# Pooled attention with a cosine router on one core: where GpSimd's drain stands, when the flagged batches are counted, and how the second pass is skipped

## The chip, the core and the metric

The kernel runs on one core of a Trainium2 chip. Its time is the device time of one execution in microseconds (us). A core has TensorE for matrix products (PE in the rows; PEld is its weight loads), VectorE (DVE), ScalarE (ACT), GpSimd (POOL) and SyncE (SP), each with its own queue of instructions, and 16 DMA engines. GpSimd's queue issues the loads of q, k, v and of the weights; SyncE's queue issues nearly all stores. A name that ends in q (POOLq, PEldq) is the sequencer of that engine, which carries out branches, waits, register loads and drains.

## The reference, cut

Attention over 8 batches, 8 heads, 576 rows of 64, in which keys and values are first averaged over groups of 8 (72 keys are left); its result is the input of a router that sends each of the 4608 rows to one of 8 experts.

```python
k_p = k.reshape(B, H, Sp, pool, D).mean(axis=3)       # Sp = 72, pool = 8
v_p = v.reshape(B, H, Sp, pool, D).mean(axis=3)
attn = softmax(scale * q @ k_p^T)
x = (attn @ v_p).transpose(0, 2, 1, 3).reshape(4608, 512)
logits = normalized(x) @ normalized(expert_emb).T / tau
expert_idx = np.argmax(logits, axis=1)                # one of 8 experts a row
gate_w = softmax(logits)[row, expert_idx]
out[mask] = gate_w[mask, None] * (np.maximum(x[mask] @ w1[e], 0.0) @ w2[e])
```

w1[e] is 512 x 1024 and w2[e] 1024 x 512.

## The kernel before, in words

A batch is one unit of work. For each of the 8 batches the kernel forms the attention, transposes its result to xt, and routes it. Before the routing is known it guesses one expert for the whole batch: `choose` (names GD, with FIND_INDEX8 as its last instruction) writes the index of the guessed expert to ix_all, `pick` (PK, L359) reads that index into a register of GpSimd's queue, and `load_w1` and `load_w2` (W1 on L343, W2 on L349) fetch that expert's weights. The products with w1 are `h_mm` (H, L707), those with w2 are `y_mm` (Y0 to Y3 of a batch, L719) and `yl_mm` (YL, the last 64 rows, L725). The rows are scaled with their gate while they leave PSUM (YE on L731, YF and YG for YL, L733 and L731) and stored (L337). W10 below means w1 of batch 0, W20 w2 of batch 0; V2 is the load of v of batch 2, Y7.2 the third product with w2 of batch 7, and so on.

Rows whose expert is not the guessed one, or whose values are out of a range, are caught by a second pass. `presence` sets this up in three steps: PR on VectorE (the range), PP on TensorE (one product of ones_m with ohb, the one-hot choices of all batches, `present`), and PX on VectorE (`extra`, 8 short instructions, L872 to L884), which write a flag for each batch (flag_i) and n_i, which is 8 if any flag is set and 0 otherwise. The program then reads n_i into a register of all five engines (L997) and runs a loop from 0 to n_i (L998). With these inputs n_i is 0 and the loop's body isn't run.

The order of the work is made before the program is built: every step is added to a plan with the engines that may run it, a busy time and a priority; the planner (`Plan.order`) places steps one at a time, by the earliest start and then the priority (for batch b it is b times PERIOD, 21, and some more, with a table of tuned corrections). GpSimd's loads have a written order of their own: V0, K0, Q0, V1, then PK0, W10, K1, Q1, W20, V2, NA0 (the root of batch 0's norms, L398), PK1, W11 and so on. Some stores wait until a load named for them has landed; `landing` holds what they wait for. While TensorE would wait early on, the planner puts products without use ahead (`keep_warm`, L813). The steps are issued in this order inside `tc.manual_schedule()`. What stands after that block is placed by a scheduler:

```python
    nc.gpsimd.drain()                                              # L996
    n_val = nc.values_load(n_i[0:1, 0:1], min_val=0, max_val=B)    # L997, all engines
    with tc.For_i(0, n_val, 1) as i:                               # L998
```

The scheduler put the drain of L996 far ahead of its place in the text: on GpSimd's queue it stands right behind the load V1 and ahead of PK0.

At the loop's end each engine jumps out of the loop, takes down the counters that it raised itself, and waits for the counters of the others; then a barrier over all engines ends the program (L1078).

Of the kernel before, what the change touches and what calls it, by code (L numbers as in the profile page):

```python
# [16 lines left out]
ALU = mybir.AluOpType  # L17
AX = mybir.AxisListType
ENG = mybir.EngineType
# [194 lines left out]
def kernel(  # L214
# [520 lines left out]
    def chunk_rows(o_b, c):  # L735
        return o_b[ts(c, 128)]
# [241 lines left out]
    for b in range(B):  # L978
        xt = Buf(xt_r)
        attention(b, b * PERIOD, xt)  # L980
        ffn(b, (b + 1) * PERIOD, xt)
    presence(B * PERIOD + 8.0)

    with tc.manual_schedule():
        order = plan.order(loads)
        first = [s for s in order if s.name in ("V0.0", "V0.1", "K0.0", "K0.1")]
        for s in first:
            s.run()
        prelude()
        for s in order:  # L990
            if s not in first:
                if s.fill:
                    keep_warm(s.fill_on, s.fill)
                s.run()

    nc.gpsimd.drain()  # L996
    n_val = nc.values_load(n_i[0:1, 0:1], min_val=0, max_val=B)  # L997
    with tc.For_i(0, n_val, 1) as i:  # L998
        f_val = nc.values_load(flag_i[0:1, ds(i, 1)], min_val=0, max_val=1)
        with tc.If(f_val > 0):  # L1000
            of = lambda t: t[ds(i, 1)].squeeze(0)
            o_b = out[ds(i * S, S)]
            xt = xt_r.tiles[0]
            attend_again(of(q), of(k), of(v), xt)
            y, o = y_r.tiles[0], y_r.tiles[1]
            nc.vector.memset(y, 0.0)
            for c in range(4):
                nc.sync.dma_start(out=chunk_rows(o_b, c), in_=y)
            put_last(o_b, y)
            w1, w2 = w1_r[0].tiles[0], w2_r[0].tiles[0]  # L1010
            with tc.For_i(0, E, 1) as e:
                p_val = nc.values_load(pick_i[0:1, ds(e, 1)], min_val=0, max_val=1)
                with tc.If(p_val > 0):
                    load_w1(e, w1)
                    load_w2(e, w2)
                    gmx = ssq_all[:, 0]
                    nc.vector.tensor_copy(out=gmx, in_=oh_x[:, :, ds(e, 1)].squeeze(2))
                    nc.vector.tensor_tensor(out=gmx, in0=gmx, in1=gate_all[:, B], op=ALU.mult)
                    hT = hT_r.tiles[0:8]
                    for w in range(8):  # L1020
                        for j in range(2):
                            p = (bank.tiles + psum.tiles)[(2 * w + j) % 4]
                            h_mm(xt, w1, w, j * HALF, (j + 1) * HALF, p)
                            h_relu(p, hT[w], j * HALF, (j + 1) * HALF, 'ACT' if j else 'DVE')
                    gl = gl_all[:, B:B + 1]
                    nc.vector.tensor_copy(out=gl, in_=gmx[64:128, 4:5])
                    for c in range(5):
                        p = (bank.tiles + psum.tiles)[c % 4]
                        if c < 4:
                            y_mm(hT, w2, c, p[:, 0:DM])  # L1030
                            scale_rows(y, p[:, 0:DM], gmx[:, c:c + 1], 'DVE')
                            dst, cols = chunk_rows(o_b, c), DM
                            nc.sync.dma_start(out=o, in_=dst)
                        else:
                            yl_mm(hT, w2, p)
                            for r in range(2):
                                rows = ts(r, 64)
                                scale_rows(y[rows, 0:DH], p[rows, ts(r, DH)],
                                           gmx[rows, 4:5] if r else gl, 'DVE')
                                nc.sync.dma_start(out=o[rows, 0:DH], in_=last_rows(o_b)[r])  # L1040
                            cols = DH
                        nc.vector.tensor_tensor(out=y[:, 0:cols], in0=y[:, 0:cols],
                                                in1=o[:, 0:cols], op=ALU.add)
                        if c < 4:
                            nc.sync.dma_start(out=dst, in_=y)
                        else:
                            put_last(o_b, y)


# [33 lines left out]
```

## Time and profile before

| | us |
|---|---|
| median of 3 runs | 209.63 (208.03 to 210.13) |
| the profiled execution | 210.25 |
| its span, from first to last recorded instruction | 208.5 |
| TensorE busy in it | 192.2 (92%) |
| VectorE, ScalarE, GpSimd busy | 140.6, 136.6, 43.0 |
| granted TensorE clock, mean over the span | 0.971 of full speed |

The profile is of one execution. Times in its rows are us from the start of the span, so an instruction "at 29.38" starts 29.38 us in. The profiled execution's own time is 1.75 us longer than its span; that part lies outside the recorded instructions. In brackets at the end of a row stands how long the engine sat idle before it and what ended that idle time.

### The profile page before, as it was taken

How to read it: one execution, taken by the hardware profiler on the slowest of the kernel's cores; microseconds unless marked ns; L12 is line 12 of the kernel's file. 1: busy time of each engine (PE TensorE's matmuls, PEld its weight loads, DVE VectorE, ACT ScalarE, POOL GpSimd, SP SyncE). 2: the span in 40 equal slices, each digit the busy share in tenths (PEclk: the TensorE clock that was granted, in tenths of full speed). 3: DMA queues.
4: the chain of work that ended last, by engine and by line, in shares of the span. 5: the costliest groups of instructions: out<-in, count | busy, mean ns of one | idle time of the engine just before them, and what ended most of it. 6: DMA issues, size and time to landing. Idle time of an engine off the chain costs nothing.

```text
span 208.5 us, 5415 instructions
## 1 busy us (share of the span) xinstructions
PE 192.2 (92%) x2080; PEld 125.2 (60%) x2081; DVE 140.6 (67%) x409; ACT 136.6 (65%) x313; POOL 43.0 (21%) x59
## 2 busy tenths in 40 slices
PE   7979989899999989999999999999999999999910
PEld 5745568447765667557765676566756676586410
DVE  2355389837896898669998897879997476242130
ACT  3004876857978779767975778469967878385410
POOL 7301603603400703006201510043000600020000
PEclk9966999999999999999999999999999999999995
DMA  4992899999999999999999999989996799950330
GB/s 56 183 183 36 137 205 212 206 207 187 207 206 176 204 211 196 209 206 210 249 208 212 177 246 242 228 173 249 239 219 232 145 218 230 267 208 3 128 104 6
DMA packets 27839, 38.71 MB, mean 186 GB/s; under 512 B 4248, under 2 KB 14488, under 8 KB 27808
## 3 DMA queue, kind: packets, MB, share of 16 engines
q0 software_dynamic: 21904, 28.85, 82.4%
q1 hardware_dynamic: 5824, 9.39, 13.3%
q8 instruction: 18, 0.29, 0.6%
q14 instruction: 13, 0.11, 0.2%
q10 hardware_dynamic: 80, 0.07, 0.1%
HBM read 61.88 MB, written 9.44 MB: 342 GB/s over the span
## 4 chain that ended last, share of the span: by engine, by line
PE 55%; DMA 24%; issue 7%; POOL 4%; DVE 4%; ACT 2%; POOLq 1%; SPq 0%; DVEq 0%; ACTq 0%
PE pb L707 20%; PE pb L719 15%; DMA kr<-in_k_dram 11%; DMA vr<-in_v_dram 10%; PE pa L589 3%; PE pa L719 3%; PE pa L707 3%; PE pa L634 3%; PE pb L378 2%; DMA out_dram<-y 2%; PE pb L725 2%; POOL vr L319 2%; PE pb L387 1%; DVE vr L448 1%; ACT y L731 1%
## 5 line engine op out<-in xcount | busy, mean ns | idle before, releaser
L707 PE MATMUL pb<-xt,w 128*128 128x288 f16 (+2 forms) x432 | 61.3, 287 | 0.9 <-DMA w<-in_moe_w_dram 0.9
L707 PEld LDWEIGHTS <-w 128*128 128x128 f16 x512 | 47.0, 98 | 16.2 <-issue 4.6
L719 PE MATMUL pb<-w,hT 128*128 128x512 f16 x224 | 52.6, 379 | 0.9 <-DMA w<-in_moe_w_dram 0.9
L597 ACT ACTIVATE at<-pa 72x576 f16<-72x576 f32 (+2 forms) x64 | 38.2, 642 | 5.2 <-PE pa L589 4.8
L719 PEld LDWEIGHTS <-hT 128*128 128x128 f16 x256 | 23.2, 97 | 26.1 <-issue 2.4
L655 ACT ACTIVATE sq<-x 128x512 f16<-128x512 f16 x40 | 25.2, 630 | 13.6 <-DVE x L370 8.7
L713 ACT ACTIVATE hT<-pb 128x288 f16<-128x288 f32 (+2 forms) x74 | 28.6, 411 | 6.9 <-PE pb L707 4.9
L731 ACT ACTIVATE y<-pb,gm_all 128x512 f32<-128x512 f32 (+1 forms) x30 | 19.0, 634 | 14.9 <-PE pb L719 11.0
L370 DVE TENSOR_TENSOR x<-pa,r_all 128x512 f16<-128x512 f32 x38 | 26.3, 691 | 2.1
L548 DVE STREAM_TRANSPOSE qT<-qq 128x576 f16<-128x576 f16 x32 | 23.2, 755 | 1.3 <-DMA qq<-in_q_dram 1.3
L398 POOL TENSOR_TENSOR ssq_all<-ssq_all,half_c 128x5 f32<-128x5 f32 x8 | 10.4, 1294 | 47.1 <-ACT sq L655 47.1
L715 DVE TENSOR_SCALAR hT<-pb 128x288 f16<-128x288 f32 (+2 forms) x34 | 14.9, 447 | 7.2 <-PE pb L707 6.9
L349 POOL DMA_DIRECT2D w<-in_moe_w_dram x8 | 5.5, 688 | 65.3 <-PE pb L725 17.0
L448 DVE TENSOR_TENSOR vr<-vr 72x2048 f16<-72x2048 f16 (+1 forms) x16 | 15.1, 942 | 5.2 <-DMA vr<-in_v_dram 5.2
L813 PE MATMUL pb<-ones_m 128*128 128x256 f16 x102 | 17.1, 314 | 1.4 <-DVE half_c L820 1.4
L589 PE MATMUL pa<-qT,kpT 32*72 32x288 f16 (+2 forms) x256 | 15.7, 295 | 0.1
L378 PEld LDWEIGHTS <-x 128*128 128x128 f16 x160 | 10.8, 97 | 6.7 <-DVE x L370 3.0
L378 PE MATMUL pb<-ident_h,x 128*128 128x128 f16 x144 | 13.5, 219 | 1.4 <-DVE x L370 1.2
L634 PEld LDWEIGHTS <-at 72*128 72x128 f16 x320 | 13.1, 98 | 1.9 <-issue 0.3
L634 PE MATMUL pa<-vpx,at 72*128 72x65 f16 x304 | 14.2, 194 | 0.0
L448 DVE TENSOR_TENSOR kr<-kr 72x2048 f16<-72x2048 f16 (+1 forms) x14 | 13.2, 944 | 1.2 <-DMA kr<-in_k_dram 1.1
L650 ACT COPY xt<-pb 128x512 f16<-128x512 f16 (+1 forms) x25 | 13.0, 536 | 0.7 <-PE pb L378 0.5
(115 smaller groups left out, 200.2 us busy)
## 6 DMA issues: line engine op xcount, KB each, us to landing
w<-in_moe_w_dram POOLq DMA_DIRECT2D x16, 1024.0 KB, 17.8
out_dram<-y SPq DMA_DIRECT2D x32, 256.0 KB, 6.1
vr<-in_v_dram POOLq DMA_DIRECT2D x7, 576.0 KB, 20.0
kr<-in_k_dram POOLq DMA_DIRECT2D x7, 576.0 KB, 18.0
qq<-in_q_dram POOLq DMA_DIRECT2D x7, 576.0 KB, 16.8
out_dram<-y SPq DMA_DIRECT2D x15, 64.0 KB, 6.3
qq<-in_q_dram POOLq DMA_DIRECT2D x2, 288.0 KB, 8.9
vr<-in_v_dram POOLq DMA_DIRECT2D x1, 512.0 KB
```

What stands on the lines that cost most here:

```text
L370: nc.vector.tensor_tensor(out=x[:, ts(i, np_)], in0=pxv[:, :, 1:129].rearrange("p a (r d) -> p a r d", d=D), in1=rv.unsqueeze(3).to_broadc ...
L378: nc.tensor.transpose(out=pt.bitcast(FP16)[:, ts(w, 128)], in_=xf[:, ts(w, 128)], identity=ident_h)
L448: nc.vector.tensor_tensor(out=t[:, :, 0:m], in0=t[:, :, 0:m], in1=t[:, :, m:2 * m], op=ALU.add)
L548: nc.vector.transpose(out=qT.tile[:, a].rearrange("p t c e -> p (t c e)")[:, cols], in_=qq.tile[:, a, cols]),
L589: nc.tensor.matmul(out=tiles[m // 2].tile[0:gs, m % 2 * 512:m % 2 * 512 + (p1 - p0) * T], lhsT=kpT.tile[ts(m, R), a, c, 0:gs], rhs=qT.tile ...
L597: nc.scalar.activation(out=t.tile[:, :, p0 * T:p1 * T].rearrange("g r (p t) -> g r p t", t=T), in_=p.tile[0:G].rearrange("g (r c) -> g r c ...
L634: nc.tensor.matmul(out=px[h // 2 // np_].tile[:, o:o + 65], lhsT=at[h // 2].tile[:, h % 2, c0:c0 + 128], rhs=vp.tile[:, h // 2, 1 + h % 2 ...
L655: nc.scalar.activation(out=sq, in_=x.tile.rearrange("p a r d -> p (a r d)"), func=AF.Square, accum_out=ssq_all[:, b, c:c + 1])
L707: nc.tensor.matmul(out=p[:, 0:c1 - c0], lhsT=w1v[:, kk, w // 2, w % 2, :], rhs=xt[:, kk, c0:c1], start=(kk == 0), stop=(kk == 3))
L713: nc.scalar.activation(out=dst, in_=src, func=AF.Relu)
L719: nc.tensor.matmul(out=p, lhsT=hT[w][:, ts(c, 128)], rhs=w2[:, w // 2, w % 2, :], start=(w == 0), stop=(w == 7))
L731: nc.scalar.activation(out=dst, in_=src, func=AF.Copy, scale=g)
```

## The change: what it does

1. The drain stands inside `manual_schedule`, as the last thing in it. On GpSimd it now comes behind the last load and the last NA, directly ahead of the reading of n_i. (The listing of instructions below leaves drains out, so this move can't be seen in it: GpSimd's rows from V1 to PK0 read alike before and after.)
2. `presence` is given a base of B * PERIOD - 200 where it was B * PERIOD + 8, so that its steps have a higher priority than most others that are ready.
3. The second pass stands under `tc.If(n_val > 0)` with its body laid out as the fall-through, and its loop runs from 0 to 8. When n_i is 0 an engine branches to the else-side of the condition, where it takes down its own counters and branches on to the end. Waits for the other engines' counters stand in that side only for SyncE, 12 of them; before, each engine had 12 or 13.
4. A hint with the branch's place ("again") is put on TensorE's queue behind the product Y7.1 (`landing["Y1"]` is overwritten batch by batch, so it is batch 7's).
5. The reading of n_i on SyncE moves ahead of the last three stores.

```diff
     def y_mm(hT, w2, c, p):
         for w in range(8):
-            nc.tensor.matmul(out=p, lhsT=hT[w][:, ts(c, 128)], rhs=w2[:, w // 2, w % 2, :],
-                             start=(w == 0), stop=(w == 7))
+            landing[f"Y{c}"] = nc.tensor.matmul(
+                out=p, lhsT=hT[w][:, ts(c, 128)], rhs=w2[:, w // 2, w % 2, :],
+                start=(w == 0), stop=(w == 7))
...
-    presence(B * PERIOD + 8.0)
+    presence(B * PERIOD - 200.0)
...
                 s.run()
-
-    nc.gpsimd.drain()
+        nc.gpsimd.drain()
+
+    with tc.issue_after(landing["Y1"].ins):
+        tc.mark_branch_hint_location("again", engines=[ENG.PE])
     n_val = nc.values_load(n_i[0:1, 0:1], min_val=0, max_val=B)
-    with tc.For_i(0, n_val, 1) as i:
-        f_val = nc.values_load(flag_i[0:1, ds(i, 1)], min_val=0, max_val=1)
...
+    with tc.If(n_val > 0, preferred_fallthrough_block=True, label="again"):
+        with tc.For_i(0, B, 1) as i:
+            f_val = nc.values_load(flag_i[0:1, ds(i, 1)], min_val=0, max_val=1)
...
```

**TensorE, batch 7's last products.** PP (the product with ohb) stands before behind YL7, the last product of all (hT are the hidden values, w the weights, pa and pb banks of PSUM):

```order
L725 LDWEIGHTS hT_102
L725 MATMUL pb_63<-w_74,hT_102 64x256
L869 LDWEIGHTS ones_m
L869 MATMUL pb_65<-ohb,ones_m 128x328
L997 TENSOR_LOAD n_i
L998 COMPARE_AND_BRANCH
```

After, it stands between Y7.0 (bank pb_64) and Y7.1 (bank pa_62):

```order
L719 LDWEIGHTS hT_99
L719 MATMUL pb_64<-w_74,hT_99 128x512
L719 LDWEIGHTS hT_102
L719 MATMUL pb_64<-w_74,hT_102 128x512
L870 LDWEIGHTS ones_m
L870 MATMUL pb_66<-ohb,ones_m 128x328
L719 LDWEIGHTS hT_103
L719 MATMUL pa_62<-w_74,hT_103 128x512
```

The hint stands between Y7.2 (bank pa_61) and Y7.3 (bank pb_63):

```order
L719 LDWEIGHTS hT_102
L719 MATMUL pa_61<-w_74,hT_102 128x512
L1082 BRANCH_PREFETCH_HINT
L719 LDWEIGHTS hT_103
L719 MATMUL pb_63<-w_74,hT_103 128x512
```

So PP went up by four products, and one instruction of the queue is new.

**VectorE, behind the gates of batch 7** (L693 is the last of them). Before, YF7, which scales half of YL7, stands ahead of the 8 instructions of PX:

```order
L693 TENSOR_TENSOR gm_all<-gm_all,gate_all 128x5
L733 TENSOR_SCALAR y_115<-pb_63,gl_all 64x256
L872 TENSOR_REDUCE pos_all<-pb_65 1x64
L875 TENSOR_SCALAR pos_all<-pos_all 1x64
L877 TENSOR_TENSOR ext<-pos_all,eb_all 1x64
L878 TENSOR_REDUCE flag<-ext 1x8
L879 SCALAR_TENSOR_TENSOR flag<-pb_65,flag 1x8
L882 TENSOR_SCALAR flag_i<-flag 1x8
L883 TENSOR_REDUCE anyf<-flag 1x1
L884 TENSOR_SCALAR n_i<-anyf 1x1
L997 TENSOR_LOAD n_i
```

After, PX stands ahead of YF7:

```order
L693 TENSOR_TENSOR gm_all<-gm_all,gate_all 128x5
L873 TENSOR_REDUCE pos_all<-pb_66 1x64
L876 TENSOR_SCALAR pos_all<-pos_all 1x64
L878 TENSOR_TENSOR ext<-pos_all,eb_all 1x64
L879 TENSOR_REDUCE flag<-ext 1x8
L880 SCALAR_TENSOR_TENSOR flag<-pb_66,flag 1x8
L883 TENSOR_SCALAR flag_i<-flag 1x8
L884 TENSOR_REDUCE anyf<-flag 1x1
L885 TENSOR_SCALAR n_i<-anyf 1x1
L734 TENSOR_SCALAR y_115<-pb_65,gl_all 64x256
L1000 TENSOR_LOAD n_i
```

PX no longer stands behind a wait for YL7.

**SyncE, the last stores.** y_112 is stored for Y7.0, y_122 for Y7.1, y_121 and y_120 for Y7.2 and Y7.3, y_115 for half of YL7. Before:

```order
L337 DMA out_dram<-y_112 128x512
L337 DMA out_dram<-y_122 128x512
L337 DMA out_dram<-y_121 128x512
L337 DMA out_dram<-y_120 128x512
L337 DMA out_dram<-y_115 64x256
L997 TENSOR_LOAD n_i
L997 ISA x2
L998 COMPARE_AND_BRANCH
```

After:

```order
L337 DMA out_dram<-y_112 128x512
L337 DMA out_dram<-y_122 128x512
L1000 TENSOR_LOAD n_i
L1000 ISA x2
L337 DMA out_dram<-y_121 128x512
L337 DMA out_dram<-y_120 128x512
L337 DMA out_dram<-y_115 64x256
L1001 COMPARE_AND_BRANCH
```

The reading of n_i moved ahead of three stores, each of which waits for its rows to be scaled.

## Rows read from the trace of the kernel before

**Rows 1.** The page: engines, granted clock, DMA, chain by engine:

```profile
PE 192.2 (92%) x2080; PEld 125.2 (60%) x2081; DVE 140.6 (67%) x409; ACT 136.6 (65%) x313; POOL 43.0 (21%) x59
...
PEclk9966999999999999999999999999999999999995
DMA  4992899999999999999999999989996799950330
...
PE 55%; DMA 24%; issue 7%; POOL 4%; DVE 4%; ACT 2%; POOLq 1%; SPq 0%; DVEq 0%; ACTq 0%
```

**Rows 2.** The drain's line, L996 (duration in ns, start in us):

```profile
L996 POOLq DRAIN  x1: 14163/14163/14163, 4.6 to 4.6; - x1
```

**Rows 3.** DMA issues of 0 to 8 us (KB each, median us to landing):

```profile
vr<-in_v_dram POOLq DMA_DIRECT2D x1, 576.0 KB, 12.2
```

**Rows 4.** The chain of waits, 0 to 30 us (start, us, what):

```profile
6.27 0.86 POOL vr L319
7.13 11.69 issue
18.82 0.48 POOLq L359
...
23.41 21.73 DMA vr<-in_v_dram
```

**Rows 5.** VectorE in order of time, 9 to 12 us:

```profile
11.13 0.17 DVE L524 FIND_INDEX8 ix_all<-mx_all,pb 128x8 uint32<-128x8 f32 x1
```

**Rows 6.** Line L343, the loads of w1 of two batches, 18 to 50 us:

```profile
L343 POOL DMA_DIRECT2D w<-in_moe_w_dram x2: 793/805/817, 20.3 to 35.9; - x2
...
DMA to landing us min/median/max: 9.0/9.0/9.0
```

**Rows 7.** Stretches: busy time of PE, PEld, DVE, ACT, POOL; PEclk; DMA share; GB/s:

```profile
18.50:21.20 2.70, 2.65 (x26) 1.09 (x25) 0.85 (x2) 1.98 (x4) 0.89 (x2) 0.95 0.00 0
...
35.90:39.90 4.00, 4.00 (x44) 2.43 (x41) 3.93 (x11) 3.44 (x9) 3.97 (x5) 1.00 1.17 209
```

**Rows 8.** TensorE in order of time, 28.5:30.2 and 40.5:42.2 us:

```profile
29.38 1.05 PE L707 MATMUL pb<-xt,w 128*128 128x256 f16 x8 [0.86 <-DMA w<-in_moe_w_dram]
...
41.73 0.81 PE L719 MATMUL pb<-w,hT 128*128 128x512 f16 x3 [0.92 <-DMA w<-in_moe_w_dram]
```

**Rows 9.** VectorE in order of time, 44.5:46.5 and 71:73 us:

```profile
45.17 1.94 DVE L448 TENSOR_TENSOR vr<-vr 72x2048 f16<-72x2048 f16 x2 [3.82 <-DMA vr<-in_v_dram]
...
71.41 1.22 DVE L448 TENSOR_TENSOR kr<-kr 72x2048 f16<-72x2048 f16 x1 [0.58 <-DMA kr<-in_k_dram]
```

**Rows 10.** The chain of waits, 185 to 209 us:

```profile
190.94 3.47 PE pb L719 x16
```

**Rows 11.** ScalarE in order of time, 193 to 208 us:

```profile
193.64 1.50 ACT L731 ACTIVATE y<-pb,gm_all 128x512 f32<-128x512 f32 x2 [1.16 <-DVE gm_all L693]
...
199.91 0.55 ACTq L337 DMA_DIRECT2D out_dram<-y  x1
```

**Rows 12.** TensorE in order of time, 193 to 200 us:

```profile
198.79 0.31 PE L869 MATMUL pb<-ohb,ones_m 128*128 128x328 f16 x1
```

**Rows 13.** VectorE in order of time, 198 to 208 us: first and last of the count:

```profile
199.31 0.47 DVE L872 TENSOR_REDUCE pos_all<-pb 1x64 f32<-1x320 f32 x1
...
200.96 0.14 DVE L884 TENSOR_SCALAR n_i<-anyf 1x1 int32<-1x1 f32 x1
```

**Rows 14.** DMA issues of 194 to 208 us:

```profile
out_dram<-y SPq DMA_DIRECT2D x4, 256.0 KB, 2.0
```

**Rows 15.** The loop's line L998, whole span: jumps and counter waits:

```profile
L998 SPq EVENT_SEMAPHORE  x21: 17/28/28, 202.2 to 204.0; - x21
...
L998 PEldq EVENT_SEMAPHORE  x14: 51/51/51, 202.0 to 207.3; - x14
```

**Rows 16.** The same line, 202 to 206.2 us: the jump on TensorE's queue:

```profile
L998 PEldq COMPARE_BRANCH  x1: 3759/3759/3759, 202.3 to 202.3; - x1
```

**Rows 17.** The end of the program, L1078:

```profile
L1078 POOLq EVENT_SEMAPHORE  x4: 17/17/17, 207.7 to 208.4; - x4
```

More of the change, by code (lines that the diff above doesn't have):

```diff
@@ new lines @@
+    with tc.If(n_val > 0, preferred_fallthrough_block=True, label="again"):
+        with tc.For_i(0, B, 1) as i:
+            f_val = nc.values_load(flag_i[0:1, ds(i, 1)], min_val=0, max_val=1)
+            with tc.If(f_val > 0):
+                of = lambda t: t[ds(i, 1)].squeeze(0)
+                o_b = out[ds(i * S, S)]
+                xt = xt_r.tiles[0]
+                attend_again(of(q), of(k), of(v), xt)
+                y, o = y_r.tiles[0], y_r.tiles[1]
+                nc.vector.memset(y, 0.0)
+                for c in range(4):
+                    nc.sync.dma_start(out=chunk_rows(o_b, c), in_=y)
+                put_last(o_b, y)
+                w1, w2 = w1_r[0].tiles[0], w2_r[0].tiles[0]
+                with tc.For_i(0, E, 1) as e:
+                    p_val = nc.values_load(pick_i[0:1, ds(e, 1)], min_val=0, max_val=1)
+                    with tc.If(p_val > 0):
+                        load_w1(e, w1)
+                        load_w2(e, w2)
+                        gmx = ssq_all[:, 0]
+                        nc.vector.tensor_copy(out=gmx, in_=oh_x[:, :, ds(e, 1)].squeeze(2))
+                        nc.vector.tensor_tensor(out=gmx, in0=gmx, in1=gate_all[:, B], op=ALU.mult)
+                        hT = hT_r.tiles[0:8]
+                        for w in range(8):
+                            for j in range(2):
+                                p = (bank.tiles + psum.tiles)[(2 * w + j) % 4]
+                                h_mm(xt, w1, w, j * HALF, (j + 1) * HALF, p)
+                                h_relu(p, hT[w], j * HALF, (j + 1) * HALF, 'ACT' if j else 'DVE')
+                        gl = gl_all[:, B:B + 1]
+                        nc.vector.tensor_copy(out=gl, in_=gmx[64:128, 4:5])
+                        for c in range(5):
+                            p = (bank.tiles + psum.tiles)[c % 4]
+                            if c < 4:
+                                y_mm(hT, w2, c, p[:, 0:DM])
+                                scale_rows(y, p[:, 0:DM], gmx[:, c:c + 1], 'DVE')
+                                dst, cols = chunk_rows(o_b, c), DM
+                                nc.sync.dma_start(out=o, in_=dst)
+                            else:
+                                yl_mm(hT, w2, p)
+                                for r in range(2):
+                                    rows = ts(r, 64)
+                                    scale_rows(y[rows, 0:DH], p[rows, ts(r, DH)],
+                                               gmx[rows, 4:5] if r else gl, 'DVE')
+                                    nc.sync.dma_start(out=o[rows, 0:DH], in_=last_rows(o_b)[r])
+                                cols = DH
+                            nc.vector.tensor_tensor(out=y[:, 0:cols], in0=y[:, 0:cols],
+                                                    in1=o[:, 0:cols], op=ALU.add)
+                            if c < 4:
+                                nc.sync.dma_start(out=dst, in_=y)
+                            else:
+                                put_last(o_b, y)
```

48 lines of the change are left out of this document (removed).

## The prediction

> **What bounds the kernel now.** I read the page first. TensorE is busy for 92% of the span, at full clock but for two slices near the start, and the chain of waits runs over TensorE for 55% and over DMA for 24% [rows 1]. So time can be won only where TensorE has nothing to do. The slices show two such places: the start, where the DMA engines fall to two tenths in the fourth slice (15.6 to 20.8 us), and the end, where TensorE falls to 1 and 0 tenths [rows 1].
>
> At the start I followed the chain. GpSimd issues V1 at 6.27, and then for 11.69 us nothing happens on it, until it reads the index of the guessed expert at 18.82 [rows 4]. That index was ready at 11.13 + 0.17 = 11.30 [rows 5]. What stands between is the drain, which lasts 14163 ns and so ends at 4.6 + 14.16 = 18.8 [rows 2]. V1 takes 12.2 us from issue to landing [rows 3], so it lands at about 6.27 + 12.2 = 18.45. I read from this that the drain waits for the transfers that GpSimd has in flight, and ends 0.3 us behind the last. It costs the DMA engines their work: from 18.5 to 21.2 us they move 0 GB/s [rows 7], because W10 is issued only at 20.3 [rows 6]. TensorE then waits for W10 (0.86 us, until 29.38) and for W20 (0.92 us, until 41.73) [rows 8].
>
> At the end, YL7's products end where PP starts, at 198.79 [rows 12], and the program ends at 208.5: 9.7 us without a needed product. In order: PP 0.31 [rows 12], YF7, the eight instructions of PX up to 200.96 + 0.14 = 201.10 [rows 13], the reading of n_i on every engine, then on TensorE's queue a jump out of the loop that takes 3.76 us from 202.3 [rows 16], then its counter waits until 207.3 [rows 15], then the barrier from 207.7 to 208.4 [rows 17]. The other engines are through with their jumps and waits by about 204.0 (SyncE's row) [rows 15]. TensorE's jump decides the end.
>
> **Part 1, the drain moves: -2.4 us.** Without it GpSimd reads the index at 11.35, as soon as it is there. From the reading to W10's issue it took 20.3 - 18.82 = 1.5 us [rows 4, 6], so W10 goes out at about 12.8 instead of 20.3, 7.5 us earlier, and K1, Q1, W20 and V2 follow at 0.8 us each [rows 6]. From 12.8 to 18.5 these loads share the DMA engines with V1, so I count not on 7.5 us but on the hole: the engines stand nearly still from about 17 to 22.5 (the slice of two tenths and the stretch of zero [rows 1, 7]), some 5.3 us. What comes later in the same queue lands up to 5.3 us earlier. W10, which landed at 20.3 + 9.0 = 29.3 [rows 6], then lands at about 24, W20 at about 36, V2 at about 40 instead of 45.15 [rows 4].
>
> What of that reaches TensorE? Its waits for W10 and W20 vanish whole: 0.86 + 0.92 = 1.78 [rows 8]. TensorE comes to W10's products at 29.38 - 0.86 = 28.5 and to W20's at 41.73 - 0.92 - 0.86 = 39.95 [rows 8], both some 4 us behind the new landings. VectorE's waits for V2 (3.82) and for K of batch 3 (0.58) [rows 9] belong to the same queue; I find nothing on TensorE that the first delays; the second stands on VectorE ahead of batch work that TensorE transposes, so I take its 0.6 as passed on. That makes 1.8 and 0.6. The lower bound is 1.0 (the second wait returns, because W11 is issued at 35.9 [rows 6] behind another reading of an index that comes only 1 us earlier). The upper bound is 4.0: TensorE is idle for 8% of the span [rows 1], which is 1.6 us of the 20 us behind V2's landing at 45.15, and all of that may be due to the late loads.
>
> The drain's new place costs nothing: the last load, w2 of batch 7, must be in before its products start at 190.94 [rows 10], and n_i comes later. If that cover were gone, only GpSimd's reading of n_i and with it the barrier would wait.
>
> **Part 2, PP and PX go up: part of the end.** PP now stands behind Y7.0. Sixteen products of 512 columns took 3.47 us [rows 10], 0.217 each, so one of 328 columns takes 0.14, and every later product is 0.14 later. Its inputs are there: batch 7's routing is over before Y7.0 starts at 190.94 (the gates, which follow the routing, are ready when ScalarE starts at 193.64 [rows 11]). PX stands behind these gates, so it runs from about 193.6; from the first start to the last end it took 201.10 - 199.31 = 1.8 us [rows 13]. n_i is ready at about 195.5 instead of 201.1. On SyncE the reading now stands ahead of the store of Y7.2. Y7.2's product ends at 194.41 + 1.73 = 196.1, and ScalarE needs 0.75 for its rows (two took 1.50 [rows 11]), so the store could go at 196.9. Before, SyncE was at its first counter 202.2 - 201.1 = 1.1 us behind n_i [rows 13, 15], so the reading is over by 196.6. The cover is 0.3 us; were it gone, the stores of Y7.2 and Y7.3 would go out that much later, ahead of a last store that leaves 3 us behind them.
>
> With PP gone from the end, YL7 ends at 198.9 + 0.1 and YF7 starts as it did. The last store goes out on ScalarE at 199.91 + 0.14 = 200.05 [rows 11], and stores take 2.0 us to land [rows 14]: 202.05. This is now what ends last.
>
> **Part 3, the skip under a condition: -3.85 us for the whole end.** TensorE reads n_i when YL7 is through, at 199.05, and jumps. From n_i to its first counter it took 202.0 - 201.1 = 0.9 [rows 13, 15]; if the jump still takes 3.76 us, it ends at 203.7. Its waits for other counters, from 206.06 to 207.3 [rows 15, 16], are gone. SyncE has the long list: it took 204.0 - 202.2 = 1.8 us for 21 semaphore instructions [rows 15] with its jumps between them. From the landing at 202.05 I count 1.5 us (some of its counters can be taken down before), so 203.55; then 0.3 for the last branch and drain (TensorE took from 207.35 to 207.7 [rows 15, 17]) and 0.8 for the barrier, from 207.7 to the end [rows 17]: 204.65 in the old time, against 208.5. The lower bound is 3.0: all of the 1.8 us, and a far branch behind it (21 semaphore instructions of 0.028 make 0.6, so 1.2 was for two jumps). The upper is 4.5: half of the list is done when the store lands.
>
> **Part 4, the hint: 0.** By Part 3 TensorE's jump ends, without a hint, at 203.7, about where SyncE is through anyway. So the hint is worth 0 to 0.3 us, and if it isn't taken up the time is 203.4 to 203.7. That it costs time is a rival.
>
> **Sum.** -2.4 - 3.85 = -6.25. The profiled execution took 210.25, with 1.75 outside its span; it should become 204.0, with a span of 202.25. It stood 0.6 above the median of the three runs, 209.63; from that median I get **203.4**.
>
> **The rivals.**
>
> *More comes from the start (201.8).* The DMA chain from 23.41 on [rows 4] moves as a whole by 5.3 us, and TensorE's short waits up to 80 us go with it: 4.0 instead of 2.4. Against it: TensorE is busy 92% [rows 1], and its own work sets the pace where loads come earlier.
>
> *The start gives nothing (205.8).* TensorE arrives earlier at the next thing that is late, such as W11, and gives the 1.8 us back: 209.63 - 3.85. For it: W11's issue depends on an index, not on the drain. Against it: W20, issued three issues or 2.4 us behind W10, was wanted only at 40.8, 18 us later, and W11's products come after W20's.
>
> *The hint does harm (207.1).* A hint makes TensorE's sequencer fetch code from elsewhere in the middle of straight code. If that displaces what comes next, TensorE waits once more for code ahead of Y7.3, and the one price in the trace for that is the jump's 3.76 us [rows 16]: 203.4 + 3.76 = 207.1. [...]
>
> *The early issues collide with VectorE (207.4).* From 12.8 to 17 GpSimd would write five loads' descriptors while VectorE works through the first batch, which TensorE waits for. If each issue held VectorE for its 0.8 us [rows 6], TensorE would start 4.0 late; it would find W10 and W20 landed, so 4.0 - 2.4 = 1.6 stands against the 3.85. The rows speak against it: W10 and W11 took 793 and 817 ns to issue, one with VectorE busy for 0.85 of 2.7 us, the other with it busy for 3.93 of 4.0 [rows 6, 7]. [...]
>
> *TensorE's clock falls (slower than before).* The page shows about 6 tenths of full clock in two slices [rows 1], some 3.5 us lost in 10.4 us if work bounds there. Today TensorE is idle or filled there, so it costs little. If the new timing of the loads leaves gaps behind which the clock falls in the bound part, each such stretch costs 3.5 us; two of them eat up the 6.25, three give 209.63 - 6.25 + 10.5 = 213.9. It decides from two on. Against it: TensorE's gaps get shorter with this change, not longer.
>
> **How the numbers follow.** Chances: the forecast 0.62, more from the start 0.13, nothing from the start 0.10, the hint does harm 0.06, collision 0.05, the clock 0.04. Of the forecast's own bounds the ends are 209.63 - 3.0 - 1.0 = 205.6 and 209.63 - 4.5 - 4.0 = 201.1. The range from 201.0 to 206.6 holds the first three cases and part of the next, 0.85 to 0.9. A measurement tells about 1% (2.1 us) from no change: faster means below 207.5. The first three cases and most of the next two lie there: 0.92. Within 1%: 0.05; slower: 0.03.
>
> **What would show it.** Right: the drain's row is short and stands at about 195 or later; W10 is issued at about 12.8; the stretch from 18.5 to 21.2 shows the DMA engines at work; TensorE's waits for w ahead of its first L707 and L719 products are gone; n_i is written about 3 us before YL7 ends; the end comes about 5.8 us behind YL7's last product instead of 9.7; the last wait is for the last store's landing and SyncE's counters. Wrong: a new wait of TensorE between 30 and 80 us for W11 or K that returns the 1.8 us (start); a gap of TensorE ahead of Y7.3 (hint); longer issues or longer VectorE instructions from 12 to 18 us (collision); a far branch on SyncE behind the last landing, which would make the end longer than 5.8 us.

## The result, and the profile after

| | before | after |
|---|---|---|
| median | 209.8 us (4 runs, 208.03 to 210.13) | 200.5 us (4 runs, 200.06 to 201.33) |
| ratio, with 95% interval | | 0.958 (0.953 to 0.964) |
| span of the profiled execution | 208.5 | 199.7 |
| its last product ends (chain of waits) | 197.87 + 1.01 = 198.9 | 192.17 + 1.01 = 193.2 |
| from there to the end | 9.7 | 6.5 |

Faster by 4.2%, about 9 us, where 6.25 were forecast; 200.5 lies 0.5 below the range's lower end. Four executions that took over 1.5% longer than the fastest of their kernel are left out here and below. The two profiled executions differ by 8.9 us (210.25 and 201.33): 5.7 of it are won before TensorE's last product ends (5.8, but for the 0.14 that the count's product now costs there), 3.2 behind it. The forecast had 2.4 and 3.85.

The last product in the chain of waits (start, us, what), before and then after:

```profile
197.87 1.01 PE pb L725 x16
```

```profile
192.17 1.01 PE pb L726 x16
```

The page of the changed kernel (engines, granted clock, DMA, chain by engine; before: [rows 1]):

```profile
PE 188.9 (95%) x2080; PEld 124.1 (62%) x2081; DVE 140.1 (70%) x409; ACT 136.6 (68%) x313; POOL 43.0 (22%) x59
...
PEclk9999999999999999999999999999999999999997
DMA  3999999999999999999999999999997599990051
...
PE 63%; DMA 22%; DVE 9%; issue 2%; POOL 1%; ACT 1%; DVEq 0%; POOLq 0%; ACTq 0%
```

The hole in the DMA engines' fourth slice is filled, as forecast. What wasn't forecast stands in the line above it: the two slices in which TensorE's clock stood at 6 tenths are gone too.

GpSimd in order of time, 4 to 45 us, in the changed kernel:

```profile
6.23 0.89 POOL L319 DMA_DIRECT2D vr<-in_v_dram  x1
13.09 0.79 POOL L343 DMA_DIRECT2D w<-in_moe_w_dram  x1 [5.98 <-DVE vpx L462]
```

The drain in its new place (line L996; duration in ns, start in us):

```profile
L996 POOLq DRAIN  x1: 2972/2972/2972, 179.9 to 179.9; - x1
```

W10 goes out at 13.1 where it went out at 20.3 [rows 6]; 12.8 was forecast. It lands 10.5 us later, at 23.6, where about 24 was forecast. The drain now ends at 182.9, two us ahead of batch 7's products with w2, and holds nobody.

The same two stretches early in the program, before and then after (columns as in [rows 7]; PEclk is the third number from the end):

```profile
12.00:15.00 3.00, 3.00 (x15) 2.13 (x15) 1.12 (x2) 0.00 (x0) 0.00 (x0) 0.50 1.03 175
15.00:18.50 3.50, 3.04 (x18) 1.73 (x15) 1.93 (x6) 0.64 (x2) 0.00 (x0) 0.50 0.50 83
```

```profile
12.00:15.00 3.00, 2.40 (x22) 1.92 (x23) 1.55 (x5) 0.64 (x2) 1.91 (x3) 1.00 1.07 182
15.00:18.50 3.50, 3.46 (x36) 1.75 (x34) 2.46 (x7) 2.00 (x4) 2.06 (x3) 1.00 1.15 194
```

Before, TensorE's granted clock was 0.50 of full speed there, after it was 1.00. The products with K of batch 0 show what that means, in order of time, before and then after:

```profile
11.90 3.57 PE L472 MATMUL pb<-kr,ident_h 72*128 72x256 f16 x16 [1.12 <-DMA kr<-in_k_dram]
```

```profile
12.14 1.92 PE L472 MATMUL pb<-kr,ident_h 72*128 72x256 f16 x16 [1.09 <-DMA kr<-in_k_dram]
```

The same 16 products, behind idle times of 1.12 and 1.09 us, took 3.57 us and 1.92 us. And the first products with w1 and with w2 (before: [rows 8], at 29.38 and 41.73, each behind a wait):

```profile
25.65 1.04 PE L707 MATMUL pb<-xt,w 128*128 128x256 f16 x8
...
37.05 1.67 PE L719 MATMUL pb<-w,hT 128*128 128x512 f16 x7
```

Neither waits now. The first starts 3.7 us earlier, not 0.9, the second 4.7 us earlier, not 1.8. At the transposes of 74.44 us, where before TensorE still waited 0.5 us for VectorE, the lead is 5.8, and it stays so to the end.

The end: the condition's line L1001 in the changed kernel (ns, first and last start; before: [rows 15, 16]), and the hint's row:

```profile
L1001 SPq EVENT_SEMAPHORE  x9: 17/17/17, 194.8 to 198.0; - x9
...
L1001 PEldq COMPARE_BRANCH  x1: 398/398/398, 192.9 to 192.9; - x1
```

```profile
L1082 PEldq BRANCH_PREFETCH_HINT  x1: 50/50/50, 186.5 to 186.5; - x1
```

TensorE's branch took 0.40 us instead of 3.76. Behind the hint, between 187 and 189 us, the DMA engines carry one 16 KB packet of instructions (queue q8); without the hint (run no_hint below) there is none from 186 to 190, so I take q8 for TensorE's queue of instructions. The hint costs TensorE 50 ns, and Y7.3 follows Y7.2 without a gap: the chain of waits has "186.99 3.45" for Y7.1 and Y7.2 and "190.44 1.73" for Y7.3. What ends last now is on SyncE, in its waits of 170 to 200 us (us in total, times, longest) and in the DMA issues of 184 to 199 us (before: [rows 14], and 1.9 for the one of 64 KB):

```profile
SPq L1001 <- SPq L1001: 3.2, 2, 2.7
```

```profile
q8 instruction: 2, 0.03, 1.1%
...
out_dram<-y SPq DMA_DIRECT2D x4, 256.0 KB, 2.0
out_dram<-y SPq DMA_DIRECT2D x1, 64.0 KB, 3.6
```

SyncE takes down one counter, then stands 2.7 us until the stores have landed, and only then goes through its list of counters, the drain and the barrier (2.1 us). The store of half of YL7 took 3.6 us to land instead of 1.9: a delay that the prediction didn't have.

### The profile page after: what moved, and what is told of

It is laid out like the page before. It is cut to its first block, busy times and chain, and to the rows that moved or that the text cites. A ratio compares the mean times of both kernels' runs of the same rounds, so it can differ in the third digit from the quotient of the medians.

```text
span 199.7 us, 5353 instructions
## 1 busy us (share of the span) xinstructions
PE 188.9 (95%) x2080; PEld 124.1 (62%) x2081; DVE 140.1 (70%) x409; ACT 136.6 (68%) x313; POOL 43.0 (22%) x59
## 4 chain that ended last, share of the span: by engine, by line
PE 63%; DMA 22%; DVE 9%; issue 2%; POOL 1%; ACT 1%; DVEq 0%; POOLq 0%; ACTq 0%
DMA vr<-in_v_dram 22%; PE pb L707 21%; PE pb L719 17%; PE pa L589 4%; PE pb L814 4%; PE pa L719 3%; PE pa L707 3%; PE pa L634 3%; PE pb L378 3%; DVE vr L448 2%; PE pb L726 2%; DVE x L370 2%; PE pb L387 1%; DVE qT L548 1%; DVE kr L448 1%
## 5 line engine op out<-in xcount | busy, mean ns | idle before, releaser
L814 PE MATMUL pb<-ones_m 128*128 128x256 f16 x102 | 16.4, 306 | 1.4 <-DVE half_c L821 1.4
L634 PEld LDWEIGHTS <-at 72*128 72x128 f16 x320 | 13.1, 98 | 1.9 <-issue 0.3
```

Of the source, the lines that this page charges most:

```text
L634: nc.tensor.matmul(out=px[h // 2 // np_].tile[:, o:o + 65], lhsT=at[h // 2].tile[:, h % 2, c0:c0 + 128], rhs=vp.tile[:, h // 2, 1 + h % 2 ...
L814: nc.tensor.matmul(out=p[:, 256:512], lhsT=ones_m[:, 0:128], rhs=ones_m[:, 0:256], start=True, stop=True)
```

## The experiments

Theory A, formed from these two traces: the drain's place is all of the start's gain (5.8 us); it is more than forecast because early weights let TensorE go at its own pace, at full clock, where before it would have waited for W10 anyway. At the end the landing of the last stores and SyncE's list decide, so the early count, the hint and the condition are not a sum: most of the gain comes as soon as TensorE's branch no longer starts behind n_i and takes 3.76 us both. The rivals are in each expectation as theory B. All ratios are to the kernel before, measured on the same chip.

| run | median us | ratio (95%) | last product ends | span |
|---|---|---|---|---|
| changed kernel | 200.5 | 0.958 (0.953 to 0.964) | 193.2 | 199.7 |
| drain_only | 203.8 | 0.976 (0.971 to 0.981) | 192.4 | 202.1 |
| before_filled | 208.7 | 0.999 (0.995 to 1.002) | 198.2 | 207.5 |
| gap_opened | 203.2 | 0.972 (0.966 to 0.978) | 195.6 | 201.6 |
| early_drain | 206.6 | 0.989 (0.983 to 0.994) | 198.5 | 205.0 |
| drain_w10 | 205.0 | 0.984 (0.980 to 0.988) | 196.9 | 203.0 |
| drain_count | 201.3 | 0.964 (0.961 to 0.968) | 193.2 | 199.9 |
| no_hint | 200.6 | 0.961 (0.958 to 0.965) | 192.4 | 199.1 |
| late_count | 200.1 | 0.961 (0.957 to 0.965) | 192.4 | 198.3 |
| late_no_hint | 202.0 | 0.969 (0.965 to 0.972) | 193.3 | 201.0 |
| held | 201.5 | 0.967 (0.963 to 0.970) | 192.6 | 199.9 |
| held_two | 201.7 | 0.968 (0.964 to 0.971) | 192.4 | 199.5 |
| late_total | 199.8 | 0.956 (0.952 to 0.961) | 193.4 | 198.6 |

The last product's end is the row of yl_mm in the chain of waits of the one profiled execution, start and length added.

**The drain alone (drain_only).**

```diff
 (kernel before)
-    nc.gpsimd.drain()          # behind the block, placed by the scheduler
+        nc.gpsimd.drain()      # last in the block
```

> Edit: the kernel before with the drain alone moved behind the last load. Theory A (the drain held the loads; everything that TensorE gained up to its last product, 5.8 us in the traces, comes from it): the end stays 9.7 us long, the last product of batch 7 ends at about 193, the time is 204.0 if TensorE's clock stays up through the first 20 us, and 206.6 if it falls there. Theory B (the drain is worth the 2.4 us of the prediction, and the other 3.4 us are something else, such as the clock's chance in one execution): 207.3.

203.8 us, and the last product ends at 192.4, 6.5 us earlier than before, with the end as long as before (9.7). Theory A holds: 5.0 us of the measured time (2.4% of 209; 4.0 to 6.0 by the interval) come from this one line. Its end shows that the jump is still there, 3839 ns on TensorE's queue:

```profile
L998 PEldq COMPARE_BRANCH  x3: 101/192/3839, 195.3 to 201.0; - x3
```

**The clock kept up in the kernel before (before_filled).** Ten products without use fill the 1.1 us in which TensorE waited for K of batch 0.

```diff
 (kernel before)
+                if s.name == "KA0.0":
+                    s.fill += 10
                 if s.fill:
                     keep_warm(s.fill_on, s.fill)
```

> Edit: the kernel before with 10 more products without use ahead of the first product with K of batch 0, where TensorE stood idle for 1.1 us and its granted clock fell to one half. Theory A: the clock stays up, TensorE comes to the first product with w1 some 2.7 us earlier and waits there 2.7 us longer (3.5 instead of 0.86), since the weights land at the same time; the time stays within 0.5 of 209.8. Theory B (the fall of the clock itself cost the kernel before 2.7 us): 207.1.

No difference that can be measured (0.999). The clock stayed up in the profiled execution, and the idle time ahead of the products with w1 grew from 0.86 [rows 8] to 2.6 us (groups of TensorE's instructions, 24 to 45 us; busy, mean ns, idle before and its releaser):

```profile
L707 PE MATMUL pb<-xt,w 128*128 128x320 f16 (+1 forms) x48 | 6.8, 288 | 2.6 <-DMA w<-in_moe_w_dram 2.6
L719 PE MATMUL pb<-w,hT 128*128 128x512 f16 x16 | 3.8, 379 | 1.1 <-DMA w<-in_moe_w_dram 1.1
```

The page's row of the granted clock, in 40 slices (before: [rows 1]):

```profile
PEclk9999999999999999999999999999999999999985
```

TensorE came to w1's products at 28.43 - 2.6 = 25.8, 2.7 us earlier, as theory A said; W10 landed 0.95 earlier (its products start at 28.43, before at 29.38), so the wait is 2.6 and not 3.5. In these traces the slow clock of the kernel before thus cost little: most of what it took from TensorE, W10 would have taken as a wait. The true size of the wait for W10 was hidden by it.

That it is quite free is not shown. The 0.999 is a mean over executions, and few of the kernel before ran at a clock as low as that of its profile (0.971 over the span): of 49 beside the runs of this table, six had a mean clock of 0.966 to 0.968, and these took 209.4 to 210.2 us, where the median of the others is 208.6.

**The clock lowered in the changed kernel (gap_opened).** The 9 products without use ahead of K's are left out, so TensorE idles longer there: 0.26 us, then 1.35.

```diff
 (changed kernel)
+                if s.name in ("GL0", "KA0.0"):
+                    s.fill = 0
                 if s.fill:
                     keep_warm(s.fill_on, s.fill)
```

> Edit: the changed kernel without the 9 products without use that stand ahead of the first product with K of batch 0, so that TensorE idles there for over 1.5 us. Theory A (with the loads early, TensorE's own pace sets the start): if the clock falls there to one half, as it did before, the time is 2.7 us longer, 203.2; if the clock doesn't fall, 200.5. Theory B (the loads still set the start): 200.5 in both cases.

The clock fell (PEclk third from the end):

```profile
12.00:15.00 3.00, 3.00 (x15) 1.81 (x12) 1.10 (x2) 0.00 (x0) 2.19 (x3) 0.50 1.19 176
15.00:18.50 3.50, 3.04 (x24) 1.85 (x23) 2.36 (x7) 0.64 (x2) 1.76 (x3) 0.56 1.05 179
```

TensorE came to w1's products at 27.87 instead of 25.65, without a wait:

```profile
27.87 1.04 PE L707 MATMUL pb<-xt,w 128*128 128x256 f16 x8
```

The time is 203.2: 2.7 longer. With early weights the fall costs what it takes; with late ones, by the six executions above, about 1 us at most. The last products' ends give the drain's worth on TensorE: 5.0 to 5.8 us with the clock up on both sides (198.2 in before_filled against 193.2 in the changed kernel and 192.4 in drain_only), and about 3.3 (198.9 - 195.6) with the clock down on both. The 5.8 of the first two traces has the clock down before and up after.

**The drain put back in the changed kernel (early_drain).**

```diff
 (changed kernel)
+                if s.name == "PK0":
+                    nc.gpsimd.drain()
                 s.run()
```

> Edit: the changed kernel with a drain put back behind the load of V of batch 1 and ahead of the reading of batch 0's index; the end stays as changed. Theory A: the start is as before, the drain lasts 14 us, the last product ends at about 198.9, and only the end's gain of 3 to 4 us is left: 206.0. Theory B (the end gave most): 203.

206.6, near theory A's 206.0. The drain lasts 13.7 us again, TensorE waits 2.1 us for w1 and 0.5 for w2, the last product ends at 198.5, and the end's gain is 1.2% or 2.4 us (1.3 to 3.5 by the interval).

```profile
L996 POOLq DRAIN  x1: 13731/13731/13731, 4.6 to 4.6; - x1
```

**What a drain waits for (drain_w10).**

```diff
 (changed kernel)
                 s.run()
+                if s.name == "W10":
+                    nc.gpsimd.drain()
```

> Edit: the changed kernel with one more drain on GpSimd, right behind the load of w1 of batch 0 (W10) and ahead of the load of K of batch 1. Theory A (a drain of GpSimd holds its queue until its transfers in flight have landed): it lasts from about 13.9 until W10 lands at 23 to 24, some 10 us, the DMA engines stand still behind it once more, K of batch 1, Q, W20 and V of batch 2 go out about 10 us later than in the changed kernel, W20 lands at about 43 where TensorE wants it at 37; the time grows by 6 or more, to 206 or above. Theory B (the drain waits only for GpSimd's own writing of descriptors, and the 14 us of before were a wait for something else): it lasts under 1.5 us and the time is within 1 of 200.5.

The drain lasts from 12.8 to 22.8, and W10 lands at 12.8 + 9.6 = 22.4 (line of the drain; then the line of W10's load):

```profile
L997 POOLq DRAIN  x1: 10052/10052/10052, 12.8 to 12.8; - x1
```

```profile
DMA to landing us min/median/max: 9.6/9.6/9.6
```

It holds the queue until GpSimd's transfer has landed, and 0.4 us more, as it did with V1. The cost, 4.5 us (5.3 by the ratios), is less than the 6 expected: K, Q and W20 went out 9.5 us later, but TensorE waited only 1.27 us for W20, and about as long for the averaged keys of batch 1 (kp), which VectorE makes from K:

```profile
33.14 0.44 PE L559 MATMUL pa<-ident_h,kp 72*128 72x72 f16 x4 [1.35 <-DVE kp L455]
```

The landing is not all that a drain can wait for. In its place in the changed kernel it lasts 2.97 us, though the last load had landed at 157.8 + 19.3 = 177.1, before the drain starts. GpSimd's last NA runs there from 179.94 to 181.14; what the 1.7 us behind it are, no run shows.

**The early count alone (drain_count).** Drain and `presence` as changed, loop from 0 to n_i as before.

```diff
 (kernel before, with the drain moved)
-    presence(B * PERIOD + 8.0)
+    presence(B * PERIOD - 200.0)
```

> Edit: the kernel before with the drain moved and the count of flagged batches put ahead of the last products, but with the loop from 0 to n_i as before: no condition, no hint. Theory A (the early count alone frees the end: TensorE's jump of 3.76 us then starts at its last product and runs beside the last store's flight, so that TensorE is ready at about 5.5 us behind its last product): 200.5 to 201.3. Theory B (the condition, which leaves the waits for other counters to SyncE alone, and the hint give the end its gain): the jump and the waits stay on the path, 203.5.

201.3, the upper edge of theory A's range, 0.3% above the other runs: the end is 6.7 us with a jump of 3.38 us that starts at 193.6, while the stores are in flight, and with every engine's 12 waits. By the medians, the condition and the hint are worth 0 to 0.8 us beside the early count.

**The hint, the late count, and both (no_hint, late_count, late_no_hint).**

```diff
 (changed kernel; no_hint and late_no_hint)
-    with tc.issue_after(landing["Y1"].ins):
-        tc.mark_branch_hint_location("again", engines=[ENG.PE])
 (changed kernel; late_count and late_no_hint)
-    presence(B * PERIOD - 200.0)
+    presence(B * PERIOD + 8.0)
```

> Edit: the changed kernel without the hint. Both theories expect TensorE's branch to take 3.76 us instead of 0.40. Theory A (the last store's landing and SyncE's list set the end): within 0.4 of 200.5. Theory B (TensorE's branch sets the end): 200.5 + 3.4 = 203.9.

> Edit: the changed kernel with the count of flagged batches behind the last products again; condition and hint stay. Theory A: n_i is ready 2.3 us behind TensorE's last product, the hinted branch takes 0.4 us, and all engines are through before SyncE: within 0.5 of 200.5. Theory B (the early count is what the end gained by): the end is longer by the 2.3 us, 202.8.

> Edit: the changed kernel with the late count and without the hint; the condition stays. Theory A: now the jump starts 2.3 us behind the last product and takes 3.76 us, so it outlasts SyncE's list by about 1.5 to 2.3 us: 202.0 to 202.8, though each of the two edits alone costs under 0.5. Theory B (the two costs add up): 200.5 + 2.3 + 3.4 = 206.2.

200.6, 200.1 and 202.0. Without the hint TensorE's branch takes 4362 ns, and nobody waits for it; with the late count it takes 477 ns, and the end is 5.9 us, shorter than the changed kernel's. Only with both undone does the branch, 3358 ns from 196.1, outlast SyncE's list, which then stands 1838 ns at TensorE's counter (no_hint, then late_no_hint, two lines):

```profile
L999 PEldq COMPARE_BRANCH  x1: 4362/4362/4362, 192.1 to 192.1; - x1
```

```profile
L999 PEldq COMPARE_BRANCH  x1: 3358/3358/3358, 196.1 to 196.1; - x1
```

```profile
L1080 SPq EVENT_SEMAPHORE  x14: 17/28/1838, 197.6 to 200.9; - x14
```

So hint and early count stand in for each other: under the condition, neither is worth anything that can be measured beside the other, and either is worth 1.5 to 1.9 us where the other is missing. That the price came out at the low end of theory A's has a likely reason: the early count has a cost of its own. The condition, too, gives something by itself. late_no_hint, which has it with neither of the two, ends 7.7 us behind its last product where drain_only takes 9.7, and stands at 0.969 against 0.976; the two intervals overlap a little, so by time its worth, some 1.5 us, is not clear of nothing.

**Why the last stores land late (held, held_two, late_total).** In the profiled executions so far with the early count the store of half of YL7 took 2.9 to 3.7 us (drain_count 2.9, gap_opened and drain_w10 3.2, changed kernel 3.6, no_hint and early_drain 3.7), in those with the late one 1.9. A fetch of 16 KB of instructions behind TensorE's branch (queue q8) lies in the changed kernel among the stores' packets: "q8 instruction: 1, 0.02, 5.7%" in the stretch from 193.9 to 195.7. It starts at 194.0, 1.1 us behind the start of the branch at 192.9, and 5.7% of 16 engines over 1.8 us make 1.6 us. The run held was to delay the branch past the stores:

```diff
 (changed kernel)
+        keep_warm(bank.tiles[1], 22)     # 22 products without use
         nc.gpsimd.drain()
```

> Edit: the changed kernel with 22 products without use on TensorE behind its last product and ahead of its reading of n_i, so that its branch comes 2.4 us later. In the changed kernel's trace the last two stores of SyncE took 4.2 and 3.6 us to land where 2.0 was usual, and a fetch of 16 KB of TensorE's instructions lay among their packets for 1.6 us. Theory A (the fetch behind TensorE's branch delays the stores, and their landing sets the end): the stores land 2.0 to 2.6 us behind their issue, and the time is 0.8 to 1.3 shorter, 199.2 to 199.7, though TensorE is done later. Theory B (the stores are late for another reason, such as the branches of the other engines): the stores stay late, and the time is 200.5 or a little more.

> Edit: as in the run held, and the two halves of batch 7's last 64 rows in two buffers, so that ScalarE's half needn't wait for VectorE's (in the changed kernel it waited 0.82 us, 0.47 of it for VectorE). Theory A: the last store goes out 0.5 us earlier and, with the stores landing in 2.0, the end is 0.5 shorter than held: 198.8 to 199.2. Theory B: the last landing isn't what sets the end: no difference to held.

Both missed: 201.5 and 201.7. TensorE's queue read n_i at 193.0, while the array was busy with the 22 products until 192.52 + 2.58 = 195.1 (TensorE in order of time; then the reading):

```profile
192.52 2.58 PE L814 MATMUL pb<-ones_m 128*128 128x256 f16 x22
```

```profile
L1001 PEldq TENSOR_LOAD <-n_i x1: 770/770/770, 193.0 to 193.0; - x1
```

So the branch came only 1.6 us later, against its last product, than in the changed kernel. The two stores of SyncE now landed in 2.0 and 1.9, and the fetch fell on ScalarE's last store instead: in the stretch from 194.9 to 196.8 the store's packets (queue q10) run out with a hole of almost 1 us in them, and the fetch lies in the same stretch.

```profile
DMA  5796934103002001000000000500000000000101
...
q10 hardware_dynamic: 70, 0.06, 15.5%
q8 instruction: 1, 0.02, 5.5%
```

That spoke for theory A but changed two things at once. In held_two the halves' two buffers gained nothing, since ScalarE still waited 0.82 us for VectorE's half; what orders the two was not looked for further. The last run delays the branch in another way:

```diff
 (changed kernel)
     def extra(p):
 ...
         nc.vector.tensor_scalar(out=flag_i, in0=flag, scalar1=0.25, scalar2=None, op0=ALU.add)
+
+    def total():
         nc.vector.tensor_reduce(out=anyf, in_=flag, axis=AX.X, op=ALU.max)
         nc.vector.tensor_scalar(out=n_i, in0=anyf, scalar1=float(B), scalar2=0.25, ...)
 ...
         add("PX", 'DVE', 1.6, base, lambda: extra(p.tile), ["PP"], uses=[p], late=0.1)
+        add("PZ", 'DVE', 0.3, B * PERIOD + 8.0, total, ["PX", f"YF{B - 1}"], late=0.1)
```

> Edit: the changed kernel with the last two instructions of the count (which write n_i) behind the scaling of batch 7's last rows on VectorE; the six ahead of them stay early. All five engines then read n_i about 1.0 us behind TensorE's last product, and branch at 1.6 to 2.0 us behind it. The run held didn't hold the branch (its reading of n_i ran ahead of the products without use), and the fetch then lay among the last store's packets. Theory A (the fetch of 16 KB behind TensorE's branch delays whatever store is in flight): it starts some 1.2 us behind the branch, that is 2.9 to 3.2 us behind the last product, when the last store's packets are through; all stores land in 2.0, the program ends about 5.2 us behind TensorE's last product (changed kernel's trace: 6.5, late count's: 5.9), time 199.2 to 199.8. Theory B (the landing of the stores doesn't depend on the branches): the end stays at 6.5, 200.5.

199.8, with an end of 5.2 us, as theory A said. The stretch from 193.9 to 196.2, in which all stores are in flight, holds no packet of q8; SyncE's store lands in 1.9, and SyncE's longest stand at its own counters is 0.5 us instead of 2.7 (DMA of that stretch; SyncE's waits):

```profile
q10 hardware_dynamic: 80, 0.07, 12.7%
q14 instruction: 2, 0.02, 2.5%
...
out_dram<-y SPq DMA_DIRECT2D x1, 64.0 KB, 1.9
```

```profile
SPq L1004 <- SPq L1004: 0.7, 2, 0.5
```

It is the fastest of the runs, by 0.7 us against the changed kernel's median, but their intervals overlap (0.952 to 0.961 and 0.953 to 0.964), so only the trace, not the time, tells them apart. That the fetch on q8 delays the stores is read from where the two stand in the traces: in the changed kernel it lay among SyncE's packets, and the last two stores took 4.2 and 3.6 us; in held it lay in a stretch with none of SyncE's packets left, in the stretches of late_total (193.9 to 196.2) and late_count (192 to 195.6) there was none, and in all three the last store took 1.9. Where it lay in the other traces with 2.9 to 3.7 us isn't shown. That the packets of queue q14 (8 KB each; I take them for the other engines' instructions) add to the delay isn't excluded, but late_total's stretch holds two of them, as the changed kernel's does.

## What the prediction had right, and where its sizes were off

**What bounds the kernel** was read rightly: the two places with time to win were the drain's 14 us and the 9.7 us behind the last product, and both gave.

**Part 1, the drain.** The mechanism held: it waits for the landing of GpSimd's transfers (14.16 us to 0.3 behind V1, 10.05 to 0.4 behind W10), W10 went out 7.2 us earlier, and the waits for W10 and W20 vanished. The term was mis-sized: -2.4 forecast, -5.0 in time for the drain alone (drain_only), -5.8 on TensorE in the changed kernel's trace. Both lie beyond the 4.0 that the prediction set as this term's bound, and that takes the time below its range. The step that failed is "TensorE comes to W10's products at 29.38 - 0.86 = 28.5". That is when it came there in one execution in which its clock stood at one half for almost 7 us. In the changed kernel it came at 25.65. The prediction had seen the two slices at 6 tenths, priced them at 3.5 us, and used them only for a rival on the slow side ("today TensorE is idle or filled there, so it costs little"). before_filled bears that sentence out but for 1 us at most, and gap_opened shows what it left out: the slow clock was cheap only because the weights came late, so taking the wait away makes the clock's state count, in either direction. The other 0.6 us, for K of batch 3, came out at 0.7 (at 74 us); 0.5 more, which the prediction didn't have, came at 58 us ahead of L559, where VectorE before stood 0.4 us waiting for a load of q.

Whether the change keeps the clock up is not shown. The instructions up to 11 us are the same; the clock fell behind a wait of 1.12 us before and stayed up behind one of 1.09 us after, and behind shorter ones (0.36 to 0.84 us, in three of them none) in the ten other traces with the same products there, early_drain's among them, which has the drain in its old place. I take the fall at this place in the profile of before for chance. The mean clocks of all executions say a little more: 0.966 to 0.990 in the 49 of the kernel before (median 0.980), 0.972 to 0.990 in early_drain, but 0.984 to 0.990 in the six of drain_only, whose end is as long as before's, and 0.994 to 0.998 in the changed kernel. With the drain early, executions ran at a lower clock more often; where in the program, no run shows.

**Part 2, the count.** PP cost 0.14 us, its inputs were there, n_i came 1.7 us behind the gates (1.8 forecast). The cover of 0.3 us on SyncE held. What was missing is what an early n_i starts: the branches, and behind TensorE's the fetch of 16 KB, at the moment when the last stores are in flight. "Stores take 2.0 us to land" failed: SyncE's last store took 3.6, and the one of 256 KB ahead of it 4.2.

**Part 3, the condition.** Forecast -3.85 for the end, -3.2 in the traces; in time -2.4 (early_drain, 1.3 to 3.5) or -3.7 (0.976 for drain_only against 0.958). The list was right (SyncE's waits, 2.1 us from the landing to the end); the landing at 202.05 in the old time was 1.2 to 1.6 us too early, and late_total, where the stores land in 2.0, has an end of 5.2 us, less than the 5.75 that the forecast's 204.65 stands for. But the gain isn't the condition's alone: drain_count has nearly all of it without, and by itself the condition took 2.0 us off the end (late_no_hint against drain_only).

**Part 4, the hint.** 0 forecast, none measured beside the early count (no_hint 0.961, changed kernel 0.958, with intervals that overlap). The branch did fall from 3.76 to 0.40 us, so the hint does what it says, off the critical path.

**The rivals.** "More comes from the start" (201.8) came nearest, but for another reason: it took the whole DMA chain to move and TensorE's short waits to go with it, and what went was one long wait that the clock had hidden. The hint did no harm: no gap ahead of Y7.3. TensorE's branches took 3.3 to 4.4 us without a hint and 0.4 to 0.5 with one. In the kernel before, one 16 KB packet of q8 starts 0.5 to 1.0 us behind the start of the jump of 3.76 us; that the jump waits for it fits, but no run shows it. The collision with VectorE didn't come: the issues from 13.1 to 17.0 us took the same 0.79, 0.85, 0.73, 0.79 and 0.86 us as those from 20.3 on before. The clock didn't fall: it was 1.00 from 12 to 18.5 us, and 0.994 over the profiled execution.

## What to carry to other kernels

A wait that the profile shows is the difference of two arrivals, and the one that waits may itself have been slow in that execution: look at the granted clock of the stretch ahead of a wait before taking the wait's length for what its removal is worth (here TensorE came to the products with w1 at 28.5 behind a clock of 0.50 and at 25.65 behind one of 1.00). A drain of GpSimd held what stood behind it in the queue until the last load had landed, for 14.16 us (kernel before) and 10.05 (drain_w10); look where the scheduler put it, not where the text has it. At the end of a program, find the last landing first: two edits that each hid the same branch of 3.3 to 4.4 us didn't add up, and behind the branch taken early a fetch of 16 KB fell among the very stores that the end waited for (3.6 us to land instead of 1.9).

## What the runs showed of the hardware

- A drain on GpSimd lasted until 0.3 us behind the landing of V1 (14.16 us, kernel before) and 0.4 behind that of W10 (10.05, drain_w10); in V1's place in early_drain it lasted 13.73. With no load in flight it still lasted 2.97 us, 1.7 of them behind GpSimd's last instruction.
- TensorE's branch to the other side of the condition, or out of the loop, took 3.28 to 4.36 us without a hint and 0.39 to 0.49 with one. In the changed kernel the hint stood at 186.5 and the branch at 192.9; a 16 KB packet on q8 came about 1 us behind the hint, and TensorE's products went on without a gap.
- In held TensorE's queue read n_i at 193.0 and branched at 193.9, while products ahead of them in the queue ran until 195.1.
- In the changed kernel's trace a 16 KB fetch of instructions on queue q8 lay among the packets of SyncE's last two stores, and these took 4.2 (256 KB) and 3.6 us (64 KB) to land. In the stretches of late_total and late_count no such fetch lay, and the store of 64 KB took 1.9.
- The clock fell to one half behind an idle stretch of 1.12 us in one execution and stayed up behind one of 1.09 us in another, with the same instructions ahead; it fell too behind 1.35 us that followed 0.26 us (gap_opened).
